# Windowed attention feeding a mixture of experts on one core: transposes two steps ahead, one mask, routing in small pieces, two experts' weights picked from the biases

## The chip, the core and the metric

The kernel runs on one core of a Trainium2 chip. A core has a matrix engine (TensorE, PE in the profile; its weight loads are PEld), a vector engine (VectorE, DVE), an activation engine (ScalarE, ACT), a general engine (GpSimd, POOL) and a queue engine that only starts transfers (SyncE, SP). Each engine runs its own instructions strictly in program order, and semaphores make one wait for another. SP, ACT and POOL can each start DMA transfers. The metric is the device time of one launch in microseconds (us); lower is better. Three timed runs give the median, and one further execution was profiled.

## The reference

Attention with a window of 32 positions to either side, over 8 batches, 8 heads, 576 positions and 64 values per head, then a mixture of 8 experts in which each of the 4608 tokens goes to one expert only:

```python
scores = scale * q @ k.T            # per batch and head, [576, 576]
scores = where(abs(i - j) <= 32, scores, -1e9)
x = softmax(scores) @ v             # then [4608, 512], heads side by side
logits = x @ w_gate + modality_bias[modality_id]
e = argmax(logits); gate = softmax(logits)[e]
out[token] = gate * (relu(x @ w1[e]) @ w2[e])
```

`w1` is 8 x 512 x 1024 and `w2` is 8 x 1024 x 512, all in fp32; `modality_bias` is 2 x 8 and spread widely, so that in these inputs the modality of a token mostly decides its expert.

## The kernel before, in words

The whole program is written out by hand in one order (`tc.manual_schedule()`), and each engine follows that order. The attention is worked in 32 steps, `it = 4*b + hp`: one batch `b` and one pair of heads `hp` in each. Eight more steps (`it` 32 to 39) have no attention. A step of the loop at L725 emits, in this order:

- at its head, the loads of batch b+2 (`load_main`, `load_rest` on the SP queue at hp 0; `load_v`, L129, on the ACT queue, at hp 1 and hp 3) and the casts to bf16 of batch b+1, nearly all on POOL (`pool_cast`, L111);
- at hp 1, `logits` of batch b-1 (L361) and `best` (L374, seven short DVE operations and an exponential);
- `scores(it+1, 0)` (L226): four matmuls of key slots 0 and 1 for the two heads, whose keys lie on partitions 0 to 63 and 64 to 127. Each slot of 128 keys meets 192 queries. The moving operand is read out of `q_t`, which holds the positions in four interleaved rows (`[P, NH, R, WP]`), so that neighbouring columns of the matmul lie 304 bytes apart. An exponential on ACT (L242) and a product with the mask on DVE (L244) follow;
- one `work(1)`, then `scores(it+1, 2)` for slots 2 and 3 and a last slot of 96 queries with a mask of its own (L250);
- at hp 0, pieces of `x_tr` (transposes of the finished batch); at hp 2, `tr_rest` (L206), the transposes of the last 64 positions;
- one `work(1)`, then `values(it)` (L253): 18 short matmuls, a reciprocal and a product on DVE that writes `xt` (L272);
- at hp 1, `place` (L397), for the first batch also `choose` (L527), and `dispatch` (L555): some twenty short DVE operations in a row, that say where each token goes; POOL then scatters the tokens to a scratch in HBM (L423);
- two more `work(1)`, and between them `tr_main(it+2)` (L215): eight transposes into one PSUM tile, a copy to `k_t` on ACT (L222) and one to `q_t` on DVE (L224). `scores` of the next step reads both and is the next thing on PE.

`work(n)` takes n units off a list. A unit is a quarter of an expert's first product (`up`, L472: eight matmuls of 256 columns and a relu on ACT) or of its second (`down`, L482: four of 512; every second one ends with DVE's `ys`, L491, and a scatter by POOL to the output, L494). A tile of 256 tokens begins with `turn` (L458): transposes, a copy on ACT (L466), the output rows on DVE. Two tiles are put on the list after each batch, of the two experts that `choose` found among the tokens of batch 0. `choose` also starts the loads of these two experts' weights on POOL's queue (L434; four transfers, read as 2 MB of fp32 each, written as 1 MB of bf16).

Before the loop, PE's first instruction is the transpose of the modality numbers (L331), which come by five DMAs on the SP queue (L325) behind the loads of batch 1. After the loop, `table` (L601, 33 short DVE operations) lays out the remaining tokens of all experts in tiles, `zero` is written behind each expert's rows, and three such tiles are worked in `tail` (L798).

PSUM is full: one score tile of two banks, one output tile of two, two transpose buffers (`ps_t`, shared by `tp`, `tpr`, `tpx`, `tpf`, `rk`), one each for `up` and `down`.

Of the kernel before, what the change touches and what calls it, by code (L numbers as in the profile page):

```python
# [31 lines left out]
def kernel(  # L32
# [27 lines left out]
    PD = 8  # L60
    WP = PD + S // R
# [16 lines left out]
    ldv = ctx.enter_context(tc.tile_pool(name="ldv", bufs=8))  # L78
# [44 lines left out]
    def load_rest(b):  # L123
        rf = ldr.tile([SR, 2, H, D], FP32, tag="rf", name="rf")
        nc.sync.dma_start(rf[:, 0], q[b, :, SM:S, :].rearrange("h s d -> s h d"))
        nc.sync.dma_start(rf[:, 1], k[b, :, SM:S, :].rearrange("h s d -> s h d"))
        Ld[b, "r"] = rf

    def load_v(b, js):  # L129
        for j in js:  # L130
            s0 = P * j if j < NM - 1 else S - P
            p0 = 0 if j < NM - 1 else P - SR
            f_ = ldv.tile([P, H, D], FP32, tag="vf", name="vf")
            nc.scalar.dma_start(f_[p0:P], v[b, :, s0 + p0:s0 + P, :].rearrange("h s d -> s h d"))
            Ld[b, "v", j] = f_
# [11 lines left out]
    def cast_rest(b):  # L147
        rb = ldr.tile([SR, 2, HD], BF16, tag="rb", name="rb")
        pool_cast(rb[:], Ld[b, "r"][:].rearrange("p u h d -> p u (h d)"))
        Ct[b, "r"] = rb  # L150

    def cast_v(b, js):
        for j in js:
            p0 = 0 if j < NM - 1 else P - SR
            pool_cast(v_t[b % 2][p0:P, j, :, 0:D], Ld[b, "v", j][p0:P])
# [3 lines left out]
    load_v(0, range(NM))  # L159
# [6 lines left out]
    WIN, WL = 192, 96  # L166
    SW = 256
    PW = 4 * SW + P

    q_t = [const.tile([P, NH, R, WP], BF16, name=f"qT{i}") for i in range(2)]  # L170
    k_t = [const.tile([P, NH, S], BF16, name=f"kT{i}") for i in range(2)]
    p_t = [const.tile([P, 2, PW], BF16, name=f"pt{i}") for i in range(2)]
    v_t = [const.tile([P, NM, H, D + 1], BF16, name=f"vt{i}") for i in range(2)]
    x_t = [const.tile([P, NM, ROW // 2], I32, name=f"xt{i}") for i in range(2)]

    def prep(i):
        nc.vector.memset(q_t[i][:, :, :, 0:PD], 0.0)
        nc.vector.memset(v_t[i][:, :, :, D:D + 1], 1.0)
        nc.vector.memset(v_t[i][0:P - SR, NM - 1, :, 0:D], 0.0)
        pv = p_t[i][:, :, 0:4 * SW].rearrange("p h (j c) -> p h j c", c=SW)  # L180
# [34 lines left out]
    def tr_main(it):  # L215
# [629 lines left out]
```

## Time and profile before

| | us |
|---|---|
| median of 3 runs (lowest, highest) | 446.59 (444.91, 449.06) |
| the profiled execution, its own time | 444.8 |
| its span, from the first to the last instruction | 443.2 |
| PE busy in it | 293.3 (66%) |
| DVE, ACT, POOL busy | 167.4, 163.4, 157.4 |
| mean granted TensorE clock | 0.85 of full |

The span is what the trace shows, and 1.6 us of the execution lie around it. [...]

### The profile page before, as it was taken

What the parts mean: (1) busy time and instruction counts of PE and PEld (TensorE: products, weight loads), DVE (VectorE), ACT (ScalarE), POOL (GpSimd) and SP (SyncE); (2) the same over time, 40 slices, a digit from 0 to 9 for tenths busy, and PEclk for the clock granted to TensorE, in tenths of its full rate; (3) what the DMA queues carried; (4) which work ended last, traced back from release to release, by engine and by line L of the source; (5) the groups of instructions that cost most, each with busy time, mean ns of one, the idle gap of its engine ahead of it and who ended that gap; (6) DMA issues with size and microseconds to landing.
All of it is one profiled execution on the core that took longest, in us unless ns stands there. A gap on an engine that the chain in (4) does not pass through costs nothing. (4 is left out here: it accounts for less than half of the span.)

```text
span 443.2 us, 7071 instructions
## 1 busy us (share of the span) xinstructions
PE 293.3 (66%) x2649; PEld 182.6 (41%) x2649; DVE 167.4 (38%) x523; ACT 163.4 (37%) x274; POOL 157.4 (36%) x216
## 2 busy tenths in 40 slices
PE   0015765406877898787888788898888877068730
PEld 0013444204644554454455445455556544045410
DVE  2015445603354455336335533644543312601110
ACT  0204354204643444454355435455535323023300
POOL 1824340823035327353642633381161611002120
PEclk9999997555988588898889888889989989569985
DMA  9999431399917823940692260240032221621020
GB/s 194 271 211 289 131 74 36 85 224 237 253 44 202 204 60 92 292 140 25 179 262 61 77 152 26 68 147 24 26 108 98 84 95 71 226 76 49 24 75 1
DMA packets 79353, 55.34 MB, mean 125 GB/s; under 512 B 49192, under 2 KB 74832, under 8 KB 79312
## 3 DMA queue, kind: packets, MB, share of 16 engines
q1 hardware_dynamic: 33184, 26.72, 22.5%
q0 software_dynamic: 8624, 18.66, 14.6%
q10 hardware_dynamic: 37504, 9.44, 10.6%
q8 instruction: 22, 0.36, 0.4%
q14 instruction: 19, 0.16, 0.1%
HBM read 54.64 MB, written 18.04 MB: 164 GB/s over the span
## 5 line engine op out<-in xcount | busy, mean ns | idle before, releaser
L478 PE MATMUL ph<-xTf,w 128*128 128x256 bf16 x608 | 87.0, 291 | 20.1 <-ACT xTf L466 14.1
L237 PE MATMUL st<-qT,kT 64*128 64x192 bf16 (+1 forms) x320 | 57.2, 459 | 57.6 <-DVE qT L224 29.6
L487 PE MATMUL py<-w,hT 128*128 128x512 bf16 x304 | 89.8, 425 | 2.2 <-DMA w<-in_moe_w_dram 1.3
L244 DVE TENSOR_TENSOR pt<-pt,mask 128x768 bf16<-128x768 bf16 x64 | 40.2, 627 | 117.6 <-ACT pt L242 117.6
L242 ACT ACTIVATE pt<-st 128x768 bf16<-128x768 f32 x64 | 51.8, 810 | 82.8 <-PE st L237 58.8
L478 PEld LDWEIGHTS <-w 128*128 128x128 bf16 x608 | 60.1, 104 | 45.9 <-issue 29.2
L494 POOL DMA_INDIRECT out_dram<-ys,ix x38 | 37.3, 983 | 111.8 <-DVE ys L491 59.5
L480 ACT ACTIVATE hT<-ph 128x512 bf16<-128x512 f32 x76 | 45.2, 595 | 85.7 <-PE ph L478 85.7
L423 POOL DMA_INDIRECT scr<-xt,di x40 | 40.9, 1023 | 72.2 <-DVE ro L566 47.2
L491 DVE TENSOR_SCALAR ys<-py,xg 128x512 f32<-128x512 f32 x38 | 28.3, 745 | 62.5 <-PE py L487 61.9
L237 PEld LDWEIGHTS <-kT 64*128 64x128 bf16 x320 | 16.0, 102 | 81.2 <-issue 68.0
L111 POOL TENSOR_SCALAR cb<-qkf 128x1024 bf16<-128x1024 f32 x30 | 31.3, 1065 | 44.5 <-PE tp L221 31.5
L487 PEld LDWEIGHTS <-hT 128*128 128x128 bf16 x304 | 29.5, 105 | 33.7 <-issue 14.6
L111 POOL TENSOR_SCALAR vt<-vf 128x512 bf16<-128x512 f32 (+1 forms) x40 | 25.7, 664 | 27.8 <-issue 15.6
L261 PEld LDWEIGHTS <-pt 128*128 128x128 bf16 x320 | 27.4, 117 | 10.0 <-issue 7.5
L466 ACT COPY xTf<-tpf 128x1024 bf16<-128x1024 bf16 x19 | 19.3, 1016 | 28.0 <-PE tpf L463 27.9
L261 PE MATMUL ot<-vt,pt 128*128 128x65 bf16 x320 | 29.3, 221 | 0.0
L266 PE MATMUL ot<-vt,pt 128*128 128x65 bf16 x256 | 27.6, 220 | 0.0
L222 ACT COPY kT<-tp 128x512 bf16<-128x512 bf16 x32 | 18.8, 586 | 22.7 <-PE tp L221 22.7
L272 DVE TENSOR_TENSOR xt<-ot,rec 128x640 bf16<-128x640 f32 x32 | 26.4, 824 | 1.2
L358 ACT COPY xTr<-tpx 128x512 bf16<-128x512 bf16 x40 | 23.1, 586 | 5.0 <-PE tpx L356 5.0
L463 PE MATMUL tpf<-ident,xg 128*128 128x128 bf16 x152 | 12.9, 233 | 18.1 <-DVE ix L468 14.6
(145 smaller groups left out, 266.0 us busy)
## 6 DMA issues: line engine op xcount, KB each, us to landing
w<-in_moe_w_dram POOLq DMA_DIRECT2D x10, 1024.0 KB, 29.9
qkf<-in_q_dram SPq DMA_DIRECT2D x16, 512.0 KB, 6.9
vf<-in_v_dram ACTq DMA_DIRECT2D x32, 256.0 KB, 4.5
qkf<-in_k_dram SPq DMA_DIRECT2D x16, 512.0 KB, 8.4
xg<-scr SPq DMA_DIRECT2D x19, 272.0 KB, 3.3
scr<-zero SPq DMA_DIRECT2D x9, 272.0 KB, 2.8
rf<-in_q_dram SPq DMA_DIRECT2D x8, 128.0 KB, 16.7
rf<-in_k_dram SPq DMA_DIRECT2D x8, 128.0 KB, 10.1
```

Of the source, the lines that this page charges most:

```text
L111: nc.gpsimd.tensor_scalar(out=o_ap, in0=i_ap, scalar1=1.0, scalar2=0.0, op0=ALU.mult, op1=ALU.add)
L237: nc.tensor.matmul(st[:, h, c0:c0 + w_], k_t[b % 2][D * h:D * h + D, hp, k0:k0 + P], q_t[b % 2][D * h:D * h + D, hp, :, q0:q0 + w_ // R].r ...
L242: nc.scalar.activation(p_ap, st[:, :, 0:2 * WIN].rearrange("p h (j c) -> p h j c", c=WIN), ACT.Exp, scale=scale)
L244: nc.vector.tensor_tensor(out=p_ap, in0=p_ap, in1=mask[:].unsqueeze(1).to_broadcast([P, 2, 2, WIN]), op=ALU.mult)
L261: nc.tensor.matmul(o_ap, pt[:, h, SW * m:SW * m + P], vt[:, m, 2 * hp + h, :], start=(m == 0), stop=(m == 0), skip_group_check=True)
L266: nc.tensor.matmul(o_ap, pt[:, h, c1:c1 + P], vt[:, m - 1, 2 * hp + h, :], start=False, stop=True, skip_group_check=True)
L423: ins = nc.gpsimd.indirect_dma_start(out=scr[:], out_offset=bass.IndirectOffsetOnAxis(ap=di[:, m:m + 1], axis=0), in_=xi[:, m, :], in_offs ...
L478: nc.tensor.matmul(ph[:, u, :], w1[:, kd, P * mi:P * mi + P], self.xT[:, kd, :], start=(kd == 0), stop=(kd == n_kd - 1))
L480: nc.scalar.activation(self.hT[:, 2 * mp:2 * mp + 2, :], ph[:], ACT.Relu)
L487: nc.tensor.matmul(self.py[:], self.hT[:, kf, P * s:P * s + P], w2[:, kf, :], start=(kf == 0), stop=(kf == n_kf - 1))
L491: nc.vector.tensor_scalar(out=ys[:], in0=self.py[:], scalar1=self.xg[:, s, HD // 2:HD // 2 + 1].bitcast(FP32), scalar2=None, op0=ALU.mult)
L494: ins = nc.gpsimd.indirect_dma_start(out=out, out_offset=bass.IndirectOffsetOnAxis(ap=self.ix[:, s:s + 1], axis=0), in_=ys[:], in_offset=N ...
```

## The change

Seven things are done together.

1. `q_t` holds the positions in their natural order, with 32 columns of zeros ahead and behind; the copy out of PSUM undoes the interleaving. All five key slots are aligned alike, and the last one is computed with 128 queries and keys padded by zeros.
2. The mask is one `[P, 192]` pattern, multiplied once in a step over all ten slots of the two heads (`masking`), after `values` of the step before.
3. `tr_main(it+2)` stands right behind `scores(it+1, 0)` instead of near the end of the step, and uses one PSUM buffer for keys and one for queries. `tr_rest` transposes queries and keys together (four transposes of 128 rows instead of eight of 64).
4. `best`, `place` and `dispatch` yield after each DVE operation, and `trickle` emits 3, 3, 2 and 3 of them at four places of a step, over some two and a quarter steps; `table` is emitted in the same way in steps 36 to 38.
5. The two experts of the in-loop tiles are the argmax of each modality's bias, known at the start: `load_ab(0)` starts two of the weight loads ahead of the loop, `load_ab(1)` the other two at step 1. `choose` is gone.
6. The modality numbers and biases are loaded first thing on the ACT queue; their transpose stands behind the first scores (`make_bias`). The values `v` of batches 1 to 7 are loaded on the SP queue. The write of the zero rows (`zp_ins`) goes from the SP queue to the ACT queue.
7. Units are not worked before step 10 (`W0`); tiles are fetched and put on the list at hp 3; the tail fetches a tile ahead of the units that remain.

The diff, cut to what the prediction speaks of:

```diff
     def load_rest(b):
+        rf = ldr.tile([P, H, D], FP32, tag="rf", name="rf")
+        nc.sync.dma_start(rf[0:SR], q[b, :, SM:S, :].rearrange("h s d -> s h d"))
+        nc.sync.dma_start(rf[SR:P], k[b, :, SM:S, :].rearrange("h s d -> s h d"))
...
+    def load_v(b, eng):
+        for j in range(NM - 1):
+            eng.dma_start(f_[:, j], v[b, :, P * j:P * j + P, :].rearrange("h s d -> s h d"))
+        eng.dma_start(l_[:], v[b, :, SM:S, :].rearrange("h s d -> s h d"))
...
     load_main(0, 0)
     load_rest(0)
-    load_v(0, range(NM))
+    mb_bc = const.tile([P, n_mod, E], FP32)
+    nc.scalar.dma_start(mb_bc[:], moe_modality_bias.partition_broadcast(P))
...
+        nc.scalar.dma_start(mid64[B * m:B * m + B, p0:p1], idv[:, s0 + p0:s0 + p1])
+    load_v(0, nc.scalar)
     load_main(0, 1)
...
-    q_t = [const.tile([P, NH, R, WP], BF16, name=f"qT{i}") for i in range(2)]
+    q_t = [const.tile([P, NH, QP + S + QP], BF16, name=f"qT{i}") for i in range(2)]
...
     def tr_main(it):
         b, hp = divmod(it, NH)
         g, l = hp // 2, 2 * (hp % 2)
-        tp = ps_t.tile([P, 2, R, P], BF16, tag="tp", name="tp")
         for u in (1, 0):
+            tp = ps_t.tile([P, R, P], BF16, tag="tp", name=f"tp{u}")
             for i in range(R):
-                nc.tensor.transpose(tp[:, u, i, :], Ct[b, g, u][:, i, D * l:D * l + P], ident[:])
-        nc.scalar.copy(k_t[b % 2][:, hp, 0:SM].rearrange("d (c r) -> d c r", r=R),
-                       tp[:, 1].rearrange("d r c -> d c r"))
-        nc.vector.tensor_copy(q_t[b % 2][:, hp, :, PD:PD + P], tp[:, 0])
+                nc.tensor.transpose(tp[:, i, :], Ct[b, g, u][:, i, D * l:D * l + P], ident[:])
+            i_ap = tp[:].rearrange("d r c -> d c r")
+            if u:
+                nc.scalar.copy(k_t[b % 2][:, hp, 0:SM].rearrange("d (c r) -> d c r", r=R), i_ap)
+            else:
+                nc.vector.tensor_copy(q_t[b % 2][:, hp, QP:QP + SM].rearrange("d (c r) -> d c r", r=R), i_ap)
...
-                    q_t[b % 2][D * h:D * h + D, hp, :, q0:q0 + w_ // R].rearrange("d r c -> d c r"),
-                    start=True, stop=True)
+                    q_t[b % 2][D * h:D * h + D, hp, P * j:P * j + w_], start=True, stop=True)
...
+    def masking(it):
+        p_ap = p_t[it % 2][:].rearrange("p h (j c) -> p (h j) c", c=SW)[:, :, 0:WIN]
         nc.vector.tensor_tensor(
+            out=p_ap, in0=p_ap, in1=mask[:].unsqueeze(1).to_broadcast([P, 2 * NM, WIN]), op=ALU.mult)
...
-    zp_ins = nc.sync.dma_start(scr[ZP:ZP + TT, :].rearrange("(s p) c -> p s c", p=P), zero[:])
+    zp_ins = nc.scalar.dma_start(scr[ZP:ZP + TT, :].rearrange("(s p) c -> p s c", p=P), zero[:])
...
+    step = [0]
+    W0 = 2 * NH + 2
     def work(n):
-        while units and (n > 0 or units[0][0].__name__ == "turn"):
+        while units and step[0] >= W0 and (n > 0 or units[0][0].__name__ == "turn"):
...
+    for i, m_ in ((0, 0), (1, n_mod - 1)):
+        nc.vector.tensor_reduce(out=pm[:, i:i + 1], in_=mb_bc[:, m_, :], axis=AX.X, op=ALU.max)
+        nc.vector.tensor_scalar(out=pe[:, i, :], in0=mb_bc[:, m_, :], scalar1=pm[:, i:i + 1], scalar2=None,
+                                op0=ALU.is_equal)
+    nc.vector.tensor_tensor(out=pe[:], in0=pe[:], in1=io_e8[:].unsqueeze(1).to_broadcast([P, 2, E]), op=ALU.mult)
+    nc.vector.tensor_reduce(out=pm[:], in_=pe[:], axis=AX.X, op=ALU.min)
...
+    def load_ab(i):
+        e_r = reg(sp_i[0:1, i:i + 1], [ET.Pool], 0, E - 1)
+        load_w(1, i, e_r)
+        load_w(2, i, e_r)
...
+    def route(b):
+        yield from best(b)
+        ranks(b)
+        yield from place(b)
+        yield from dispatch(b)
...
     scores(0, 0)
     scores(0, 2)
+    masking(0)
+    cast_main(0, 1, split=True)
+    load_ab(0)
+    make_bias()
     for it in range(n_it + 2 * NH):
...
+        if it == 1:
+            load_ab(1)
         st = None
         if hp == 1 and rb is not None:
             st = logits(rb)
+            chain[0] = route(rb)
         if it + 1 < n_it:
             scores(it + 1, 0, st)
+        if hp == 2 and it + 2 < n_it:
+            tr_rest(b + 1)
+        if it + 2 < n_it:
+            tr_main(it + 2)
+        trickle(3)
         work(1)
         if it + 1 < n_it:
             scores(it + 1, 2)
         if hp == 0 and rb is not None:
+            x_tr(rb, 0)
             x_tr(rb, 1)
+        trickle(3)
         work(1)
+        if live:
+            values(it)
         if hp == 0 and rb is not None:
             x_tr(rb, 2)
+        if it + 1 < n_it:
+            masking(it + 1)
+        trickle(2)
         work(1)
         if hp == 0 and rb is not None:
             x_tr(rb, 3)
+            x_tr(rb, 4)
+        trickle(3)
         work(1)
+        if hp == 3 and rb is not None:
+            trickle(99)
             for t in got[rb]:
                 t.fetch()
             for t in got[rb]:
                 enqueue(t)
+            if rb == B - 1:
+                chain[0] = table()
+    trickle(99)
...
     def tail(idx, first):
+            t.fetch()
+            work(len(units))
             load_w(1, i % 2, e_r, cond=(c_r == 1))
+            load_w(2, i % 2, e_r, cond=(c_r == 1))
             enqueue(t)
```

## Rows read from the trace of the kernel before

**Rows 1.** The page's span in 40 equal slices: PE's busy tenths

```profile
PE   0015765406877898787888788898888877068730
```

**Rows 2.** Timeline of the start: start us, us, engine, line, operation, [idle before <-releaser]

```profile
20.18 0.19 POOL L302 CAST iof<-ioi 128x8 f32<-128x8 int32 x1
...
22.32 0.56 POOL L345 MEMSET zero<- 128x544 int32 x1
...
31.03 0.21 PE L331 MATMUL midp<-ident,midr 40*128 40x40 bf16 x1 [31.03 <-DVE midr L327]
...
34.84 0.81 PE L237 MATMUL st<-qT,kT 64*128 64x192 bf16 x4
```

**Rows 3.** Timeline of `xt`, written once a step: steps 0, 3, 9 and 31

```profile
43.13 0.82 DVE L272 TENSOR_TENSOR xt<-ot,rec 128x640 bf16<-128x640 f32 x1
...
61.09 0.82 DVE L272 TENSOR_TENSOR xt<-ot,rec 128x640 bf16<-128x640 f32 x1
...
124.99 0.82 DVE L272 TENSOR_TENSOR xt<-ot,rec 128x640 bf16<-128x640 f32 x1
...
332.47 0.82 DVE L272 TENSOR_TENSOR xt<-ot,rec 128x640 bf16<-128x640 f32 x1
```

**Rows 4.** Timeline, steps 5 to 7: the stall at the weight loads

```profile
80.98 0.82 PE L237 MATMUL st<-qT,kT 64*128 64x192 bf16 x4 [6.38 <-DVE qT L224]
...
84.61 0.86 POOL L438 DMA_DIRECT2D w<-in_moe_w_dram  x1
...
86.22 14.05 ACTq L134 DMA_DIRECT2D vf<-in_v_dram  x3
...
101.17 0.98 PE L237 MATMUL st<-qT,kT 64*128 64x192 bf16 x6 [12.34 <-ACT pt L242]
```

**Rows 5.** The view of tile `w` to 130 us: issue to landing of four loads

```profile
DMA to landing us min/median/max: 26.3/29.9/33.5
```

**Rows 6.** Windows: length, busy (count) of PE PEld DVE ACT POOL, PEclk, DMA, GB/s

```profile
0.00:31.00 31.00, 0.00 (x0) 0.00 (x0) 2.90 (x15) 3.37 (x3) 14.11 (x50) 1.00 1.03 222
31.00:72.00 41.00, 27.48 (x271) 17.92 (x273) 21.41 (x47) 18.49 (x31) 13.52 (x16) 0.99 0.62 158
...
135.00:345.00 210.00, 176.39 (x1680) 107.85 (x1678) 97.64 (x305) 99.03 (x172) 87.68 (x99) 0.88 0.42 118
```

**Rows 7.** Windows again, one of 2 us that holds a score group

```profile
80.00:82.00 2.00, 0.82 (x4) 0.25 (x4) 0.86 (x6) 0.17 (x1) 1.70 (x2) 0.50 0.33 122
```

**Rows 8.** Waits of PE alone from 135 to 345 us: total, times, longest

```profile
PE st L237 <- DVE qT L224: 12.6, 15, 1.7
PE ph L478 <- ACT xTf L466: 8.4, 6, 1.5
PE st L237 <- ACT pt L242: 5.7, 4, 2.0
```

**Rows 9.** Timeline of PE in step 27, at full clock

```profile
298.85 0.22 PE L261 MATMUL ot<-vt,pt 128*128 128x65 bf16 x2
...
299.40 1.03 PE L478 MATMUL ph<-xTf,w 128*128 128x256 bf16 x8
...
300.27 0.61 PE L221 MATMUL tp<-ident,cb 128*128 128x128 bf16 x8
...
302.05 0.81 PE L237 MATMUL st<-qT,kT 64*128 64x192 bf16 x4 [0.31 <-DVE qT L224]
```

**Rows 10.** Groups of instructions, shapes apart: busy us, mean ns, idle before

```profile
L244 DVE TENSOR_TENSOR pt<-pt,mask 128x768 bf16<-128x768 bf16 x64 | 40.2, 627 | 117.6 <-ACT pt L242 117.6
...
L224 DVE COPY qT<-tp 128x512 bf16<-128x512 bf16 x32 | 13.5, 421 | 20.0 <-ACT kT L222 19.7
...
L381 DVE TENSOR_TENSOR oh<-lo,mx 128x40 f32<-128x40 f32 x8 | 1.6, 200 | 0.3
```

**Rows 11.** Timeline of the end: after the table, and the last scatter

```profile
390.20 1.01 PE L463 MATMUL tpf<-ident,xg 128*128 128x128 bf16 x8 [14.58 <-DVE ix L468]
...
427.71 0.97 POOL L494 DMA_INDIRECT out_dram<-ys,ix  x1 [1.75 <-POOLq L814]
```

More of the change, by code (lines that the diff above doesn't have):

```diff
@@ L405, in place @@
                 start=False, stop=(m == NM - 1), skip_group_check=True)
+    def place(b):
+        xi, ohb, rk = x_t[b % 2], Ct[b, "oh"], Ct[b, "rk"]
         pos = rt.tile([P, E], FP32, tag="pos", name="pos")
@@ L556, in dispatch @@
+    got = {}
+    def dispatch(b):
         cm = small.tile([P, 2, E], FP32, tag="cm", name="cm")
@@ L718, with trickle, run_all @@
     n_it = NH * B
-    got = {}
+    chain = [None]
+    def trickle(n):
+        while chain[0] is not None and n > 0:
+            if next(chain[0], chain) is chain:
+                chain[0] = None
+            n -= 1
+    def run_all(g):
+        for _ in g:
+            pass
+    def route(b):
[3 more added lines that the diff above has]
+        yield from dispatch(b)
     tr_rest(0)
@@ L759 @@
         if hp == 0 and rb is not None:
+            x_tr(rb, 0)
             x_tr(rb, 1)
-        if hp == 2 and it + 2 < n_it:
-            tr_rest(b + 1)
+        trickle(3)
         work(1)
+        if live:
+            values(it)
         if hp == 0 and rb is not None:
             x_tr(rb, 2)
-        if live:
-            values(it)
-        if hp == 1 and rb is not None:
-            place(rb)
-            if rb == 0:
-                choose()
-            got[rb] = dispatch()
+        if it + 1 < n_it:
+            masking(it + 1)
+        trickle(2)
         work(1)
@@ L775 @@
             x_tr(rb, 3)
-        if it + 2 < n_it:
-            tr_main(it + 2)
+            x_tr(rb, 4)
+        trickle(3)
         work(1)
-        if hp == 0 and rb is not None:
-            x_tr(rb, 4)
-        if hp == 2 and rb is not None:
+        if hp == 3 and rb is not None:
+            trickle(99)
             for t in got[rb]:
                 t.fetch()
-        if hp == 3 and rb is not None:
             for t in got[rb]:
                 enqueue(t)
-    tab_steps = table()
-    while units:
-        work(1)
-        for _ in range(4):
-            next(tab_steps, None)
-    for _ in tab_steps:
-        pass
+            if rb == B - 1:
+                chain[0] = table()
+    trickle(99)
     tab, pen_i = T["tab"], T["pen"]
@@ L804, in tail @@
             load_w(1, i % 2, e_r, cond=(c_r == 1))
-            t.fetch()
+            load_w(2, i % 2, e_r, cond=(c_r == 1))
             enqueue(t)
-            work(len(units))
-            load_w(2, i % 2, e_r, cond=(c_r == 1))
+        work(len(units))
         for n in range(4):
```

244 lines of the change are left out of this document (115 added, 129 removed).

## The prediction

> **What bounds the kernel now.** I read the page's 40 slices first. PE is idle for nearly three of them at the start, has a hole in slices 7 to 9 and one near the end; between them it is busy eight to nine tenths [rows 1]. So there are four terms: start, early hole, main loop, end.
>
> At the start PE's first instruction waits 31 us for the modality numbers, and all other PE work is queued behind it; the first scores begin at 34.84 [rows 2]. In the hole, ACT needs 14.05 us to issue three loads of `v` while the weight loads fill the DMA engines; its exponential is behind them, and PE waits 12.34 us for that [rows 4]. In step 6 PE also waited 6.38 us for the copy of q, which stood behind `place`, `choose` and `dispatch` on DVE [rows 4]. In the loop a step takes (332.47 - 124.99)/22 = 9.43 us [rows 3]. From 135 to 345 us PE is idle for 210 - 176.39 = 33.6 us, 1.55 in a step of 9.69 (210/9.69 = 21.7 steps); ACT is busy for 99.03/21.7 = 4.6 us of a step, DVE 4.5, POOL 4.0 [rows 6]. [...] At the end PE is idle 14.58 us while DVE works the table [rows 11].
>
> **The change, part by part**, against the profiled span of 443.2 us.
>
> *Start.* The transpose of the modality numbers leaves PE's head. What is late next: ACT now has to issue `zp_ins` ahead of its first copy of k, and that waits for `zero`, which POOL has done at 22.32 + 0.56 = 22.9 [rows 2]; behind ACT's wait stand all copies of k and exponentials. DVE has the choice of experts ahead of its first copy: some 12 small operations at 0.20 [rows 10] behind an index table that POOL makes at 20.18 + 0.19 [rows 2], so 22.8. Both say 22.9 (20 if POOL's queue gets shorter by the two masks and the cast that leave it, 28 if `v` lands later). From there two rounds of transposes and copies through two PSUM buffers take some 2.4 us: first scores at 25.3, not 34.84. From first scores to `xt` of step 0 it was 43.13 - 34.84 = 8.3; less 2 for faster scores and one wait for q, plus some 0.5 as ACT's cast of the second half of k now stands there: 6.7. `xt` of step 0 comes at 32 (29 to 37).
>
> *Steps 1 to 9.* They took (61.09 - 43.13)/3 = 5.99 each before any routing [rows 3]. Less 0.9 for scores and 0.6 for the wait for q (both below): 4.5, bounds 4.0 and 5.5. `xt` of step 9 is at 32 + 9 x 4.5 = 72.5. Do the transfers allow it? In the first 31 us come 31 x 222 GB/s = 6.9 MB, about two batches (3.54 MB each), so 15 us a batch [rows 6]. The weights take at most 33.5 us from 84.61 [rows 4, 5], in which one whole batch comes too: 33.5 - 15 = 19. Three batches and the weights are 64 us, and the first third of batch 3 makes 69: it just fits. I add 2 us for order, since SP's fetch of the first tiles is queued behind batch 3's `v`: 74.5 (0 to +12). Before it was 124.99, with 8 units done by then that are now still to do. `work` is gated to step 10, so the weights have until then. The issue of `v` goes from ACT, where it cost 14.05, to SP, where only loads and fetches stand behind it.
>
> *Main loop, steps 10 to 31.*
> (a) Scores. Four matmuls of 192 columns take 0.81 at full clock [rows 9] and 0.82 at a granted clock of 0.50 [rows 4, 7], six 0.98 [rows 4]. What doesn't change with PE's clock isn't the array; I take it to be the strided read of q. `up` streams 8 x 256 columns in 300.27 - 299.40 = 0.87, or 0.42 ns a column, plus a tail of 1.03 - 0.87 = 0.16 [rows 9]. At that rate, with both heads at once, the groups take 0.32 and 0.38; one head after the other, 0.48 and 0.60; if it isn't the stride, nothing is gained. The saving is 1.09, 0.71 or 0; I take 0.9 a step.
> [...] No run here shows a contiguous score matmul.
> (b) Waits. Of PE's listed waits, 12.6 us for q, 8.4 for `xTf`, 5.7 for the exponential [rows 8], the first goes (12.6/21.7 = 0.58 a step): the copy now has a whole step's time, and routing is no longer ahead of it in one piece. The exponential gets the eight transposes as cover beside one unit; half of its 0.26 and half of the 0.39 for `xTf` go. Together -0.9, bounds 0 and -1.55 (all idle time).
> (c) Clock. [...] As far as lows come from the waits that go: -0.4 (0 to -1.1).
> (d) Added. DVE's copy of q now reads PSUM with a stride: from 0.42 as before to, at most, the 0.63 of the larger mask product [rows 10]. One mask of 1920 elements against two of 768 and a short one: at most 0.627 x 2.5 = 1.57 against 1.25 and more, so nothing to speak of. DVE stays under 5 us, POOL loses little, ACT is unchanged in sum, but at hp 0 five copies of `xTr` and one of `xTf` meet, and the two PSUM buffers change hands 17 times in a batch instead of 13. I add 0.3 (0 to 1).
> 9.43 - 0.9 - 0.9 - 0.4 + 0.3 = 7.5 (bounds 5.8 and 10.4; I hold 6.5 to 8.8 for likely, as PE's work alone is near 6). 22 x 7.5 = 165: `xt` of step 31 at 239.5.
>
> *Steps 32 to 39.* They took 390.20 - 14.58 - 332.47 = 43.1 [rows 3, 11] with 28 units (16 tiles make 124, 96 were done before). Now 32: + 4 x 0.87, and about 5 less for waits on tiles and low clock: 41.6 (38 to 46). The table's operations lie beside units.
>
> *End.* The 14.58 go (at least 9 of them); some 1 us of register loads on PE stays, and 4 units are left, 3.5. From the first tail tile to the last scatter 427.71 - 390.20 = 37.5, and 443.2 - 427.71 = 15.5 after it [rows 11], both as before.
>
> Sum: 74.5 + 165 + 41.6 + 1 + 3.5 + 37.5 + 15.5 = 338.6; with 1.6 around the span 340.2, where the profiled execution had 444.8. The median of the runs is 0.4% above that one: 341.
>
> **Rivals.**
> *A, the loop stays coupled:* q's wait goes but PSUM hand-over and ACT's crowd at hp 0 take its place, a step of 8.6. 22 x 1.1 more: 365. For: buffers change hands more often; against: ACT is busy 4.6 of 9.7 [rows 6].
> *B, the early transfers are late:* the weights crowd out batches 1 and 2, as they held up `v` in [rows 4]; steps 4 to 9 wait, some 12 us: 353. Against: the 69 us above.
> [...]
> *D, nothing comes of it:* gains at start and end are eaten by a step slower than before (at some 12.3 us, should routing in pieces hold up masks and values at each place): within 1%.
>
> **How the numbers follow.** Forecast 0.70, A 0.15, B 0.10, C 0.03, D 0.02. The likeliest is 341; its parts (start and early steps -10 to +15, loop -22 to +28, rest -7 to +7) added in squares make 316 to 372, which takes in B and most of A. About 1% is what a measurement here can tell from no change: faster 0.95, within 1% 0.02, slower 0.03.
>
> **What would show it.** First scores near 25, behind ACT's wait for `zero`; `xt` of step 9 near 74 and no wait of ACT on its own DMA issues; score groups near 0.35 and 0.4; no wait of PE for `qT`; `xt` 7.5 apart; PE's idle before the tail under 4 us. The forecast is wrong if score groups stay at 0.8, if the granted clock falls below 0.8 in the loop, or if steps 4 to 9 wait for loads.

## The result, and the profile of the changed kernel

The changed kernel took 348.74 us (median of 4 runs, 346.44 to 350.13) where the kernel before, beside it, took 446.66: a ratio of 0.780, with a 95% interval of 0.774 to 0.786. The forecast was 341, with a range of 316 to 372. The profiled execution has a span of 348.4 us against 443.2, that is 94.8 less.

The page's 40 slices first, PE's busy tenths and the granted clock:

```profile
PE   0114776535779897988889798798398688888810
...
PEclk9999998655599999999999999999699999999975
```

A slice is now 8.7 us. PE is idle for most of the first three, 24 us of 26, where before it was 32 of 33 [rows 1]; the hole before the tail is gone; the early hole is still there, in slices 7 to 10, and the granted clock is at its lower level, 0.50, in slices 9 to 11 (of the 480 half-microsecond windows from 60 to 300 us 397 show 1.00, 78 show 0.50 and 5 a value between). There is a new hole, in slice 29 (244 to 253 us, step 31): ACT's copy, and PE's wait for it.

```profile
248.14 1.01 ACT L478 COPY xTf<-tpf 128x1024 bf16<-128x1024 bf16 x1 [3.07 <-remote]
...
249.21 1.87 PE L490 MATMUL ph<-xTf,w 128*128 128x256 bf16 x8 [5.43 <-ACT xTf L478]
```

The transposes that this copy reads had ended at 243.77. The experiments come back to this ("The changed kernel again").

`xt`, the last DVE operation of a step's values, divides the span as in [rows 3]. Its timeline: steps 0, 7, 8, 9, 23 and 31.

```profile
36.33 0.82 DVE L272 TENSOR_TENSOR xt<-ot,rec 128x640 bf16<-128x640 f32 x1
...
64.66 0.82 DVE L272 TENSOR_TENSOR xt<-ot,rec 128x640 bf16<-128x640 f32 x1
...
79.08 0.82 DVE L272 TENSOR_TENSOR xt<-ot,rec 128x640 bf16<-128x640 f32 x1 [2.19 <-DMA scr<-xt,di]
...
85.65 0.83 DVE L272 TENSOR_TENSOR xt<-ot,rec 128x640 bf16<-128x640 f32 x1
...
194.04 0.82 DVE L272 TENSOR_TENSOR xt<-ot,rec 128x640 bf16<-128x640 f32 x1
...
253.88 0.82 DVE L272 TENSOR_TENSOR xt<-ot,rec 128x640 bf16<-128x640 f32 x1
```

Steps 0 to 7 are (64.66 - 36.33)/7 = 4.05 us apart, but step 8 comes 14.4 after step 7, and step 10, in which the first units are worked, 13.2 after step 9. Against [rows 3], 39.3 of the 94.8 us are won up to step 9, 39.3 in the 22 steps from 9 to 31 (a mean of 7.65 a step, not 9.43, step 10 among them), and 16.2 behind it.

Windows of the loop, columns as in [rows 6], and PE's longest waits in the same stretch (total, times, longest):

```profile
105.00:243.00 138.00, 121.21 (x1465) 82.91 (x1462) 91.17 (x225) 86.72 (x152) 70.76 (x78) 1.00 0.53 151
```
```profile
PE tpx L349 <- DVE qT L227: 3.9, 4, 1.0
PE tp L222 <- DVE kT L214: 3.3, 4, 0.8
```

The wait of the scores for `qT`, 12.6 us in [rows 8], has left the list. The two waits that lead it now are of transposes for a PSUM buffer that a copy on DVE has to set free; together they are 7.2 us, 0.38 a step. The granted clock is 1.00 where it was 0.88; PE is idle 0.88 us of a 7.26 us step (16.8 us in 138/7.26 = 19 steps), not 1.55. A score group in this stretch, four and then six matmuls, where [rows 9] had 0.81 for the four:

```profile
156.57 0.34 PE L238 MATMUL st<-qT,kT 64*128 64x192 bf16 x4
...
158.93 0.40 PE L238 MATMUL st<-qT,kT 64*128 64x192 bf16 x6
```

The end: the first tail tile's transposes, without a wait where [rows 11] had 14.58, and the last scatter.

```profile
298.33 0.61 PE L475 MATMUL tpf<-ident,xg 128*128 128x128 bf16 x8
```
```profile
333.02 0.97 POOL L506 DMA_INDIRECT out_dram<-ys,ix  x1 [1.76 <-POOLq L860]
```

### The profile page after: what moved, and what is told of

It reads as the page before. It is cut to its first block, busy times and chain, and to the rows that moved or that the text cites. A ratio compares the mean times of both kernels' runs of the same rounds, so it can differ in the third digit from the quotient of the medians.

```text
span 348.4 us, 6915 instructions
## 1 busy us (share of the span) xinstructions
PE 242.0 (69%) x2617; PEld 165.7 (48%) x2617; DVE 173.8 (50%) x464; ACT 162.4 (47%) x274; POOL 149.9 (43%) x195
## 5 line engine op out<-in xcount | busy, mean ns | idle before, releaser
L490 PE MATMUL ph<-xTf,w 128*128 128x256 bf16 x608 | 81.8, 278 | 22.4 <-ACT xTf L478 9.8
L499 PE MATMUL py<-w,hT 128*128 128x512 bf16 x304 | 79.4, 383 | 3.5 <-DVE ys L503 2.2
L222 PE MATMUL tp<-ident,cb 128*128 128x128 bf16 x256 | 25.5, 243 | 26.0 <-DVE kT L214 12.9
L250 DVE TENSOR_TENSOR pt<-pt,mask 128x1920 bf16<-128x1920 bf16 x32 | 37.8, 1182 | 2.4 <-ACT pt L245 2.4
L271 DVE RECIPROCAL rec<-ot 128x10 f32<-128x10 f32 x32 | 7.0, 219 | 58.9 <-PE ot L266 29.6
L222 PEld LDWEIGHTS <-cb 128*128 128x128 bf16 x256 | 17.2, 108 | 33.8 <-DVE kT L214 14.3
L238 PE MATMUL st<-qT,kT 64*128 64x192 bf16 (+1 forms) x320 | 26.2, 261 | 9.9 <-DVE lo L363 3.6
L227 DVE COPY qT<-tp 128x512 bf16<-128x512 bf16 x32 | 22.0, 689 | 17.4 <-PE tp L222 16.4
L261 PE MATMUL ot<-vt,pt 128*128 128x65 bf16 x320 | 24.3, 202 | 5.7 <-POOL vt L110 5.3
L261 PEld LDWEIGHTS <-pt 128*128 128x128 bf16 x320 | 22.4, 103 | 7.6 <-issue 1.3
L225 ACT COPY kT<-tp 128x512 bf16<-128x512 bf16 x32 | 18.8, 586 | 15.4 <-POOL le L606 11.6
L478 ACT COPY xTf<-tpf 128x1024 bf16<-128x1024 bf16 x19 | 19.2, 1012 | 13.2 <-PE tpf L475 10.1
```

What stands on the lines that cost most here:

```text
L222: nc.tensor.transpose(tp[:, i, :], Ct[b, g, u][:, i, D * l:D * l + P], ident[:])
L250: nc.vector.tensor_tensor(out=p_ap, in0=p_ap, in1=mask[:].unsqueeze(1).to_broadcast([P, 2 * NM, WIN]), op=ALU.mult)
L261: nc.tensor.matmul(o_ap, pt[:, h, SW * m:SW * m + P], vt[:, m, 2 * hp + h, :], start=(m == 0), stop=(m == 0), skip_group_check=True)
L490: nc.tensor.matmul(ph[:, u, :], w1[:, kd, P * mi:P * mi + P], self.xT[:, kd, :], start=(kd == 0), stop=(kd == n_kd - 1))
L499: nc.tensor.matmul(self.py[:], self.hT[:, kf, P * s:P * s + P], w2[:, kf, :], start=(kf == 0), stop=(kf == n_kf - 1))
```

## The experiments

They ran in three groups, each beside the kernel before on its own chip, which took 450.28, 441.92 and 441.08 us there. So ratios are compared, and the third group has the changed kernel itself once more.

**The changed kernel again.** No edit. It ran in the last group, but belongs first, since the others are read by it.

> The changed kernel as it is, run beside the three that follow. In its first profile a batch of the loop took 29.3 us, with 9.3 to 9.7 us for the last step of each batch; in the four kernels of the last comparison (table, weights, casts of v, biases) a batch took 26.4 us or 27.3, with 6.1 us for that step, whatever had been edited, and they ran on another chip. Theory (that difference is the chip's and no edit's): the changed kernel itself shows either 29.3 us and a ratio near 0.78, or 26.4 us a batch and 330 to 334 us, a ratio of 0.75 to 0.757, and the three kernels beside it show the same batch. Rival (each of those edits freed the loop in its own way): 29.3 us here and less in the others.

331.62 us (329.98 to 335.09), ratio 0.758 (0.752 to 0.764): the second form of the theory, with a ratio just above the 0.757 put down. The same program is 17 us faster on this chip, where the kernel before gained 5.6. A batch takes 26.5 us and not 29.3, as in three of the four kernels of the second group. `xt` of steps 9 and 31 in this trace:

```profile
85.68 0.83 DVE L272 TENSOR_TENSOR xt<-ot,rec 128x640 bf16<-128x640 f32 x1
...
235.44 0.82 DVE L272 TENSOR_TENSOR xt<-ot,rec 128x640 bf16<-128x640 f32 x1
```

Step 23, the last of its batch, in the first trace and in this one: GpSimd's last scatter of five, the last of the values' 18 matmuls, then DVE's reciprocal that waits for it.

```profile
190.27 0.97 POOL L435 DMA_INDIRECT scr<-xt,di  x1 [0.30 <-issue]
```
```profile
190.31 0.20 PE L266 MATMUL ot<-vt,pt 128*128 128x65 bf16 x1
```
```profile
193.78 0.22 DVE L271 RECIPROCAL rec<-ot 128x10 f32<-128x10 f32 x1 [4.47 <-PE py L499]
```
```profile
183.73 0.97 POOL L435 DMA_INDIRECT scr<-xt,di  x1 [0.30 <-issue]
```
```profile
183.77 0.20 PE L266 MATMUL ot<-vt,pt 128*128 128x65 bf16 x1
```
```profile
184.00 0.22 DVE L271 RECIPROCAL rec<-ot 128x10 f32<-128x10 f32 x1 [1.96 <-PE ot L266]
```

In the second trace DVE starts at once when the values end, at about 183.97. In the first it starts 3.3 us after them, and 3.2 to 3.6 us late in the last step of each of the four batches from step 12 to 27, while GpSimd issues the scatters. ACT is held up alike: its copy in step 31 begins 4.4 us after the transposes that it reads [the row at 248.14]. There the profile names the releaser "remote": it finds no instruction of this core that released it. This name stands on ACT or DVE in the first trace and in all four of the first group, and in none of the eight traces of the other two groups. The scatters themselves run alike (0.97 us each, 1.27 apart). What holds up the signal the traces don't show. From step 9 to 31 the two traces differ by 168.23 - 149.76 = 18.5 us, 2.9 in each of those four batches and 5.8 in the last one; up to step 9 (85.7 in both) and behind step 31 (94.5 and 94.9) they agree. The kernels of the first group have the long last step of a batch too (9.1 us with q strided, for 9.3 in the first trace and 6.1 in this one), so they are compared with 0.780; the second and third group have the short one and are compared with 0.758.

**q strided again.**

```diff
-q_t = [const.tile([P, NH, QP + S + QP], BF16, ...
+q_t = [const.tile([P, NH, R, (QP + S + QP) // R], BF16, ...
...
-    q_t[b % 2][D * h:D * h + D, hp, P * j:P * j + w_], ...
+    q_t[b % 2][D * h:D * h + D, hp, :, P // R * j:(P * j + w_) // R].rearrange("d r c -> d c r"),
```

> The changed kernel with q stored again in four interleaved rows, so that the right-hand side of every score matmul is strided and the copy of q out of PSUM is contiguous. All else as in the changed kernel: both heads in one group of four and one of six matmuls. Theory (the stride is what made the old score groups long, and they stand on TensorE's path): the groups of four and of six go from 0.34 and 0.39 us to about 0.80 and 0.97, so some 1.0 us per step, in the 22 steps from 10 to 31 alone 23 us (the first ten steps wait for transfers and hide it): 372 us, from 366 to 378. Rival 1 (it was the one-head-after-another order that was slow, not the stride): groups stay under 0.5 and the time within 4 us of 348.7. Rival 2 (the stride costs TensorE time, but the loop is bound elsewhere): groups long and the time under 358.

360.32, ratio 0.801 (0.797 to 0.804): 0.021 x 446.7 = 9 us lost. Added to 348.7 that is 358, the second rival's bound and not the theory's 366 to 378. The groups are just as the theory has them:

```profile
162.36 0.81 PE L239 MATMUL st<-qT,kT 64*128 64x192 bf16 x4
...
164.72 1.02 PE L239 MATMUL st<-qT,kT 64*128 64x192 bf16 x6
```

So the stride alone made them long, by 0.81 + 1.02 - 0.34 - 0.40 = 1.09 us a step: the order of the heads has no part in it. But from step 9 to 31 it costs 177.5 - 168.2 = 9.3 us, 0.42 a step. The steps at hp 1 and hp 2 grow by 1.1 and 0.6 us; the one that holds the late signal and the one behind it don't grow at all (9.1 for 9.3, and 5.3). On a chip without that lateness this wasn't tried.

**Contiguous q alone, in the kernel before.**

```diff
-q_t = [const.tile([P, NH, R, WP], BF16, ...
+q_t = [const.tile([P, NH, R * WP], BF16, ...
...
-    q_t[b % 2][D * h:D * h + D, hp, :, q0:q0 + w_ // R].rearrange("d r c -> d c r"),
+    q_t[b % 2][D * h:D * h + D, hp, R * q0:R * q0 + w_],
```

> The kernel before with one part of the change alone: q stored in natural order, so that the right-hand sides of the score matmuls are contiguous, and the copy of q out of PSUM strided. Transposes, routing, masks, weights and table as before. Theory (parts add up): about 1.0 us per step off TensorE in the 22 steps from 10 to 31, and little in the steps that wait for transfers: 446.6 - 23 = 424, from 418 to 432; the wait for qT grows by the 0.27 us by which the strided copy is longer. Rival (before, the loop had slack from its waits, so that a shorter group only lengthens a wait): 440 to 447.

437.27, ratio 0.971 (0.967 to 0.975): 13 us won, a little over half of what was expected, between theory and rival. Windows and PE's wait, from 135 to 345 us as in [rows 6, 8]:

```profile
135.00:345.00 210.00, 154.22 (x1662) 108.01 (x1681) 103.81 (x308) 98.68 (x172) 89.95 (x99) 0.89 0.40 114
```
```profile
PE st L238 <- DVE qT L224: 24.6, 14, 3.8
```

PE is busy 154.22 us, 22 less than before, but waits 24.6 for `qT`, 12 more. The work that left PE had been cover for the copy of q, and the copy itself is longer (0.69 us for 0.42, some 4 of the 12 us over 14 waits). In this trace the 22 steps from 9 to 31 take 207.5 us, as many as before [rows 3]: on PE the loop's work shrank and its waits grew by as much. What the traces show as won is 6.3 us up to step 9 (118.67 for 124.99) and 1.6 behind the loop. The kernel before has no trace on this chip, where it took 3.6 us longer, so how much of the 13 is the loop's stays open. That this part counts in full with the transposes out of the way isn't shown either.

**Transposes at their old place.**

```diff
-        if it + 2 < n_it:
-            tr_main(it + 2)
         trickle(3)
...
             x_tr(rb, 3)
+        if it + 2 < n_it:
+            tr_main(it + 2)
```

> The changed kernel with the transposes of q and k, and those of the rest rows, at their old places: tr_main(it + 2) behind the fourth x_tr near the end of the step, tr_rest behind the second half of the scores. Theory (the wait for qT stands between TensorE and the next scores): the wait of the scores for qT comes back with about 0.6 us per step, and with it some of the idle time between units: 22 steps by 0.6 to 0.9 = 13 to 20 us, so 365 (360 to 372). Rival (with the routing spread, VectorE is free when the copy comes, and the copy is done in time wherever it stands): within 4 us of 348.7.

393.23, ratio 0.866 (0.862 to 0.871): 0.086 x 446.7 = 39 us lost, more than twice what was expected, and the largest of the parts that were undone. (The profiled execution took 397.81, at a mean clock of 0.868 where three others had 0.89 to 0.90, so its terms are somewhat too large.) Windows of the start and the loop of this kernel, and of the start of the changed one, then a wait in step 1 of this kernel:

```profile
0.00:100.00 100.00, 39.81 (x467) 31.48 (x468) 47.34 (x113) 34.97 (x57) 42.79 (x73) 0.83 1.03 229
110.00:290.00 180.00, 142.18 (x1541) 97.80 (x1563) 97.07 (x242) 96.46 (x165) 79.28 (x85) 0.89 0.43 121
```
```profile
0.00:100.00 100.00, 46.01 (x569) 33.77 (x570) 51.23 (x135) 40.98 (x68) 52.03 (x83) 0.83 1.07 241
```
```profile
45.04 0.50 PE L238 MATMUL st<-qT,kT 64*128 64x192 bf16 x4 [2.86 <-DVE qT L227]
```

(`tr_rest` went back behind the second half of the scores as well.) A step from 0 to 7 takes (85.2 - 35.7)/7 = 7.1 us and not 4.05; from 36 to 86 us PE waits for `qT` six times, 14.2 us in all, where the changed kernel waits 0.6. From step 9 to 31 it is (301.9 - 101.1)/22 = 9.1. PE's longest waits from 110 to 290 us:

```profile
PE tp L222 <- ACT kT L225: 10.6, 5, 2.3
PE st L238 <- DVE qT L227: 9.5, 7, 3.1
```

So the wait for `qT` comes back with 0.48 us a step (180/9.1 = 19.7 steps), near the theory's 0.6, but more is lost where the transposes wait for ACT's copy of k to set a buffer free. The granted clock of the loop is 0.89, as in the kernel before, where the changed kernel has 1.00. From 115 to 240 us PE has six waits of 1.9 to 4.4 us, and the clock's six stretches at 0.50 each begin in one of them or shortly behind it, so waits and low clock come together. In the first trace the clock's falls near 65.5 and 246.5 us lie in waits of PE too, of 3.13 and 5.43 us.

**Routing in two pieces.**

```diff
-            chain[0] = route(rb)
         if it + 1 < n_it:
             scores(it + 1, 0, st)
+        if st is not None:
+            run_all(best(rb))
...
             masking(it + 1)
+        if st is not None:
+            ranks(rb)
+            run_all(place(rb))
+            run_all(dispatch(rb))
```

> The changed kernel with the routing of a batch in two pieces again: the choice of the expert right behind the first half of the scores, ranks, places and dispatch behind the values of the same step. Theory (a block of some 20 small VectorE operations in the hp = 1 step holds up the copies of q and the masks): about 5 us of VectorE work in one piece, of which 2 to 4 us per batch come onto the path, 6 batches inside the loop: 361 (356 to 370). Rival (the block is covered by the units): within 4 us of 348.7. A second rival: the scatters leave a step earlier and the casts of v behind them on GpSimd with them, so that it is faster, 340 to 345.

365.26, ratio 0.809 (0.805 to 0.813): 0.029 x 446.7 = 13 us lost, the theory's size. A batch takes 34.2 us and not 29.3, and the step that grows is the one after the block, hp 2: 10.9 for 7.4. There, GpSimd's first scatter, ACT's and PE's wait:

```profile
191.95 1.00 POOL L435 DMA_INDIRECT scr<-xt,di  x1 [6.30 <-issue]
```
```profile
200.67 0.60 ACT L492 ACTIVATE hT<-ph 128x512 bf16<-128x512 f32 x1 [6.44 <-remote]
```
```profile
202.22 0.58 PE L222 MATMUL tp<-ident,cb 128*128 128x128 bf16 x4 [4.88 <-ACT xTf L478]
```

The relu waits for a releaser that the profile names "remote", 4.95 to 6.44 us, four times in the loop; in the row shown, the matmuls that it reads had ended at 195.44. GpSimd issues the scatters meanwhile, and PE waits 4.88 behind it. So the size was right, but the wait is not the theory's: DVE's block is done at 192.3 (`thr`, its last short operation), and the stall is a late signal during the scatters, as in the first trace. Whether the 13 us are there on a chip without that lateness wasn't tried, and so the cause stays open.

**The table behind the loop.**

```diff
             if rb == B - 1:
-                chain[0] = table()
+    chain[0] = table()
     trickle(99)
```

> The changed kernel with the table of the tail worked out in one piece behind the loop's last units, where the kernel before had most of it, and not spread between them from step 35 on. Theory (the table's small VectorE operations, some 40, and the register loads behind them stand between the last units and the tail when nothing covers them): the 14.58 us of idle time of the kernel before come back in large part, +9 to +14, a ratio to the kernel before of 0.805 (0.798 to 0.814) where the changed kernel has 0.781. Rival (the tail waits for its weights anyway, so the table is hidden behind a transfer): ratio under 0.787.

343.05, ratio 0.777 (0.769 to 0.785). Against 0.780 it would look like nothing; a batch takes 26.5 us here, so it stands against 0.758 and is a loss, 0.0187 x 441 = 8 us. Step 31 ends at 235.4 in this trace and in that of the changed kernel's second run, and the last scatter begins at 326.15 and 315.08: 11 us, the theory's. PE's wait in front of the last four units, ahead of the first tail tile:

```profile
285.26 1.86 PE L490 MATMUL ph<-xTf,w 128*128 128x256 bf16 x8 [8.14 <-DVE g L725]
```

Behind it the four units run at a granted clock of 0.51 (285 to 291 us) and take 1.3 to 1.9 us each and not 1.03, which makes most of the rest of the 11.

**Weights at steps 4 and 5.**

```diff
-    load_ab(0)
...
-        if it == 1:
-            load_ab(1)
+        if it in (4, 5):
+            load_ab(it - 4)
```

> The changed kernel with the weights of the two experts asked for at steps 4 and 5 and not at the start and at step 1. In the changed kernel the 16 DMA engines are full from 26 to 100 us (busy share above 1 in both stretches), and the ninth and the eleventh step came 14.4 and 13.2 us after the one before. Theory (the weights, 8 MB read by the second step, push back the loads of batch 2, and these end the waits of steps 8 to 10): step 9 ends at about 76 and not 85.7, and as the weights then land at about 85 to 90, close to the first unit, the gain is kept in part: ratio 0.765 (0.755 to 0.775). Rival 1 (every byte is wanted by step 10 in either order): the wait moves from the steps to the first units, ratio 0.776 to 0.787. Rival 2 (the weights come too late and the units stall as in the kernel before): ratio above 0.79.

333.66, ratio 0.760 (0.754 to 0.766), the changed kernel's 0.758: no gain. First the changed kernel, in its first trace DVE's index for the scatters of batch 0 and the first of these, in its second the cast of v ahead of them; then this kernel, the first scatter, the values of step 8, and `xt` of steps 8 and 9.

```profile
59.72 0.17 DVE L426 TENSOR_SCALAR di<-dr 128x5 int32<-128x5 f32 x1
...
67.89 1.10 POOL L435 DMA_INDIRECT scr<-xt,di  x1 [0.29 <-POOL xt L433]
```
```profile
63.99 1.05 POOL L110 TENSOR_SCALAR vt<-vf 128x1024 bf16<-128x1024 f32 x1 [8.94 <-DMA vf<-in_v_dram]
```
```profile
60.33 1.10 POOL L435 DMA_INDIRECT scr<-xt,di  x1 [6.80 <-DVE rec L271]
...
68.47 0.19 PE L261 MATMUL ot<-vt,pt 128*128 128x65 bf16 x1 [2.14 <-POOL vt L110]
...
80.30 0.82 DVE L272 TENSOR_TENSOR xt<-ot,rec 128x640 bf16<-128x640 f32 x1 [10.22 <-DMA scr<-xt,di]
...
86.87 0.82 DVE L272 TENSOR_TENSOR xt<-ot,rec 128x640 bf16<-128x640 f32 x1
```

86.9 and not 76: the gain that the theory wanted doesn't come. But the weights matter all the same. In the changed kernel the index is ready at 59.9, but GpSimd waits with the cast of batch 2's v, whose load lands late beside the weights, until 63.4, has casts of q and k behind it, and starts the scatters at 67.9. Here that cast comes at 47.4, the scatters start at 60.3 and the values of step 8 at 68.5, for 75.3. Then `xt` waits 10.22 us for these scatters, which now run beside the weights: the three whose landing the trace has took 13.8 to 18.6 us, for 4.6 to 6.7 in the changed kernel's second trace. So one wait takes the place of the other. Weights out of the way of both the loads and the scatters weren't tried. Read against 0.780 the ratio alone would have confirmed the theory.

**Casts of v ahead of the scatters.**

```diff
         if hp == 1 and nb is not None:
             cast_rest(nb)
-            cast_v(nb, 0)
+            cast_main(nb, 1)
         if hp == 2 and nb is not None:
-            cast_main(nb, 1)
-        if hp == 3 and nb is not None:
+            cast_v(nb, 0)
             cast_v(nb, 1)
             cast_v(nb, 2)
```

> The changed kernel with the casts on GpSimd in another order: those of q and k a step earlier at most, those of v all at the third step of a batch, ahead of the five scatters of the batch before, where two of the three stood behind them. Theory (the values of step 8 waited 5.1 us for a cast of v that stood behind five scatters of 1.28 us, though its load had landed, and steps 10 and the last of every batch look alike): 4 to 8 us, nearly all of it ahead of step 11: ratio 0.767 (0.76 to 0.773). Rival 1 (the loads land late anyway and the wait takes their name): ratio 0.777 to 0.785. Rival 2 (a cast of v waits for its load ahead of casts of q and k, and holds up the transposes): slower, ratio above 0.787.

338.33, ratio 0.767 (0.762 to 0.773), against 0.758 a loss of 4 us: a batch takes 27.3 us and not 26.5, the step at hp 1 8.0 and not 7.2. First the changed kernel's step 8: the fifth scatter of batch 0, the cast of v behind it, the values, and `xt`; then `xt` of step 8 in this kernel.

```profile
73.17 0.97 POOL L435 DMA_INDIRECT scr<-xt,di  x1 [0.31 <-issue]
74.17 1.07 POOL L110 TENSOR_SCALAR vt<-vf 128x1024 bf16<-128x1024 f32 x1
```
```profile
75.29 0.21 PE L261 MATMUL ot<-vt,pt 128*128 128x65 bf16 x1 [5.07 <-POOL vt L110]
```
```profile
80.09 0.82 DVE L272 TENSOR_TENSOR xt<-ot,rec 128x640 bf16<-128x640 f32 x1 [10.24 <-DMA scr<-xt,di]
```

The wait for the cast (5.07) is gone, and another takes its name: `xt` of step 8 writes the buffer that the scatters of batch 0 read, and waits 10.24 us until they have landed, at 80 us, among full transfers. In the changed kernel that wait was 2.19 [the row at 79.08].

**Biases at step 2.**

```diff
-    make_bias()
 for it in range(n_it + 2 * NH):
...
+        if it == 2:
+            make_bias()
```

> The changed kernel with the modality biases worked out at step 2 and not in the start, where their five VectorE operations (31.6 to 35.3 us) stood between the first mask and the first copies of q of the loop, and held a PSUM buffer of the transposes for 2.4 us. Theory (the start is a chain, and what leaves it comes off the end): xt(0) at 33 and not 36.3, ratio 0.773 (0.77 to 0.776). Rival (the steps from 4 on wait for transfers, so that an earlier start ends in a longer wait): xt(0) earlier all the same, step 9 where it was, ratio 0.778 to 0.785.

332.51, ratio 0.755 (0.750 to 0.760): no difference from 0.758. `xt` of steps 0 and 9:

```profile
33.67 0.82 DVE L272 TENSOR_TENSOR xt<-ot,rec 128x640 bf16<-128x640 f32 x1
...
86.20 0.82 DVE L272 TENSOR_TENSOR xt<-ot,rec 128x640 bf16<-128x640 f32 x1
```

The start is 2.6 us shorter than the 36.33 of the changed kernel, and step 9 stands where it was: the rival's outcome, but not by its wait alone. The biases now lengthen step 2 to 8.3 us (3.4 in the changed kernel), so that step 3 is already late, at 48.1 for 45.7.

**Three buffers for the attention output.**

```diff
-x_t = [const.tile([P, NM, ROW // 2], I32, name=f"xt{i}") for i in range(2)]
+x_t = [const.tile([P, NM, ROW // 2], I32, name=f"xt{i}") for i in range(3)]
...
-        xi, ohb, rk = x_t[b % 2], Ct[b, "oh"], Ct[b, "rk"]
+        xi, ohb, rk = x_t[b % 3], Ct[b, "oh"], Ct[b, "rk"]
```

> The changed kernel with three buffers for the attention output x_t where it has two. With the casts of v ahead of the scatters, the normalisation of step 8 waited 10.24 us for the scatters of batch 0, which read the buffer that it writes and landed near 80 us among the full transfers; in the changed kernel that wait is 2.2 us, since the values of step 8 came late themselves behind the casts of v. Theory (two waits end at nearly the same time, so that taking away one gives what lies between them): xt(8) 1.5 to 2.5 us earlier, and the time by 0 to 2.5 less than the changed kernel beside it. Rival (the buffer is the only bound): xt(8) near 70 and 8 us less.

330.73, ratio 0.757 (0.752 to 0.762), 0.9 us under the changed kernel beside it: within the theory and within the measurement's spread. `xt` of step 8 comes at 77.0; the values still wait for the cast.

**Three buffers and the casts of v first.** Beside the three buffers:

```diff
         if hp == 2 and nb is not None:
             cast_main(nb, 1)
-        if hp == 3 and nb is not None:
             cast_v(nb, 1)
             cast_v(nb, 2)
```

> Three buffers for x_t, and the second and third cast of v one step earlier, ahead of the five scatters on GpSimd. Theory (both waits of step 8 are gone, and what is late next are the loads of batch 3 and the first fetch, near 80): xt(8) at 70 to 73 and not 79, xt(9) at 77 to 80 and not 86, and as TensorE isn't idle for 10 us there its clock stays at the higher level; 5 to 9 us less than the changed kernel beside it. Rival 1 (all bytes wanted by step 10 end at the same time whatever waits for them): xt(8) earlier, xt(11) where it was, within 2 us of the changed kernel. Rival 2 (the casts delay the scatters by 1.7 us in every batch, and these the fetches): slower by 1 to 4 us.

331.79, ratio 0.762 (0.755 to 0.769): nothing won, as the first rival has it, though `xt` of step 8 comes at 70.2. Step 9 comes 12.5 us later. Its DVE, GpSimd and PE:

```profile
75.43 6.11 DVE L384 TENSOR_TENSOR oh<-iof,mi 128x40 f32<-128x40 f32 x1
```
```profile
75.83 2.08 POOL L110 TENSOR_SCALAR cb<-qkf 128x1024 bf16<-128x1024 f32 x2
...
79.44 2.04 POOL L110 TENSOR_SCALAR cb<-qkf 128x1024 bf16<-128x1024 f32 x2
```
```profile
82.60 0.21 PE L403 MATMUL rk<-ohb,tri 128*128 128x40 bf16 x1 [7.01 <-DVE ohb L388]
```

A DVE operation that takes 0.20 us elsewhere lasts 6.11, beside six casts in a row on GpSimd (four of them in the rows), from 75.83 to 81.48; PE waits 7.01 behind it. So a third wait was ready to end at nearly the same time. `xt` of step 9 is 3 us earlier, at 82.7, and the loop afterwards gives nothing more.

**And the biases at step 2 with them.**

> As the kernel with three buffers and the casts of v a step earlier, and the modality biases at step 2 and not in the start. Theory (what the start gives is lost again in the steps that wait for transfers): xt(0) 2 to 3 us earlier, the time within 1.5 us of the kernel without this part. Rival (with the waits of step 8 gone the early chain counts): 2 to 4 us less than it.

329.48, ratio 0.757 (0.751 to 0.762): 2.1 us under the changed kernel beside it and 2.3 under the one without this part, the rival's size in the medians; but the intervals overlap with both, so it can't be called faster. `xt` of step 9 is at 84.7, 2 us later than without it, so no early chain shows in the trace.

## Why the prediction was right, and which step failed

The forecast was 2% under the time, and the time lies well inside the range. In part that is luck, as told under the loop. Its terms for the first chip against the trace of the changed kernel:

| term | forecast | measured |
|---|---|---|
| `xt` of step 9 | 74.5 | 85.65 |
| 22 steps to step 31 | 165 | 168.2 |
| from there to the first tail tile | 41.6 + 1 + 3.5 = 46.1 | 298.33 - 253.88 = 44.45 |
| tail, to the last scatter | 37.5 | 333.02 - 298.33 = 34.7 |
| after it | 15.5 | 348.4 - 333.02 = 15.4 |

*Start: right in place, short in size.* First scores came at 26.64 for 25.3, behind ACT's first copy of k:

```profile
25.06 0.58 ACT L225 COPY kT<-tp 128x512 bf16<-128x512 bf16 x1 [11.60 <-POOL le L606]
```

The profile names POOL's `le` for this wait, but ACT issues the write of `zero` at 24.62, right ahead of the copy and right after POOL has made `zero` (24.04 + 0.55), so it is the wait that was forecast, 1.7 us later. `xt` of step 0 came at 36.33 for 32: the biases' DVE operations were moved into this chain, which the step didn't count, and moving them out gives 2.6 of the 4.3 us back (biases at step 2).

*Steps 1 to 9: the step that failed.* "It just fits. I add 2 us for order" was mis-sized: 11 us more at step 9, near the +12 of its upper bound. Up to step 7 the steps ran at 4.05, under the forecast 4.5. The bytes came about as counted: the forecast has three batches and the weights in by 64 us, and GpSimd casts batch 2's first v at 63.45 (63.99 in the second trace). What the step put at nothing is the work between that landing and the values of step 8, all in GpSimd's order: casts of q and k, the five scatters of batch 0, which had waited for GpSimd since 59.9, and the other casts of v. That makes 75.29 - 63.45 = 11.8 us. Then `xt` waits 2.19 more until the scatters have landed. So rival B had the size and a part of the cause: weights asked for 15 us later bring the values of step 8 forward by 6.8 us, but step 9 stays at 86.9, since the scatters then land late. Taken away one by one the waits replace each other (weights later, casts first, three buffers), and with the last two both gone DVE's wait at GpSimd comes third.

*Loop: right in the sum, by luck in part.* The 168.2 us hold the late signals, for which the forecast has no term. On the chip without them the same 22 steps took 149.8, 15 us less than the forecast's 165 and 6.8 a step (the kernel before was 5.6 us faster there too). So the parts (a) to (d) together were put too low, and a loss that nobody foresaw filled the gap.

*(a) Scores: 0.9 a step, measured 1.06 to 1.09 on PE* (0.34 and 0.39 or 0.40 us, the "both heads at once" end of the bound), settled by the strided q. Six matmuls took 0.39 or 0.40 us, where the forecast's estimate was 0.38 with both heads at once and 0.60 one after the other. Four took 0.34 us, and 0.81 with the stride. The strided four took as long at either clock (0.81 and 0.82 in the kernel before); the contiguous four take 0.34 at a granted clock of 1.00 and 0.51 at 0.50 (first trace, at 60.64 us). On the end of the kernel it is worth 0.42 a step on the first group's chip.

*(b) and (c), waits and clock: -1.3 a step, measured about -1.5* by the transposes at their old place (9.1 against 7.65, of which some 0.2 to 0.3 is the longer execution that was profiled). The forecast had them as two terms; in that trace they come together. No run shows the clock's -0.4 by itself; the granted clock of the loop went from 0.88 to 1.00, and is 0.89 with the transposes at their old place. Of the waits only 0.48 a step is for `qT`, and the largest is for a PSUM buffer, which the forecast had as rival A. The 9.69 us step by which the forecast divides stands in no row; with the 9.43 of [rows 3] the wait for q is 0.57 a step and not 0.58. The same waits cost 3 us a step in steps 0 to 7, where only 0.6 was put down.

*(d) Added: +0.3.* The copy of q takes 0.69 us, just over the bound of 0.63, the mask at most what was bounded. That the routing in pieces saves 13 us had no term of its own. Two sums of the forecast are a little off, without effect: the lower bound of a step is 5.7 and not 5.8, and the range's upper end 373.5 and not 372.

The parts don't add: undone singly, stride, transposes, routing and table cost 9 + 39 + 13 + 8 to 11, some 70 us (the table on another chip than the rest), where all together won 98, and contiguous q alone gave 13 where its undoing costs 9. What one part takes away is cover for the wait of another.

*End: right.* The 14.58 are gone, and the table behind the loop brings 8.14 of them back.

Rival A (a step of 8.6) did not come: the step is 7.65; its hand-over of PSUM buffers is there, but at 0.38 us a step. Nor did D, whose step of 12.3 is the one at which the 446.6 - 341 = 105.6 us of the forecast are used up in 22 steps (7.5 + 4.8), nor C of the chances, a slower loop: the granted clock is 1.00 in it, for 0.88 before.

## What to carry to other kernels

Work taken off the bounding engine pays in full only if nothing was waiting under its cover: contiguous q alone doubled the wait for the copy of q (24.6 us for 12.6) and, in its trace, left the loop as long as it was. In a stretch bound by transfers count what has to happen after a load has landed, and the scatters too: where they stand in the issuing engine's order and which buffer their landing sets free. And expect two or three waits to end within a few microseconds of each other. Run the unedited kernel in the same group: without it, the table would have passed for hidden here, and weights, casts and biases for gains.

## What the hardware showed that was not expected

**The same program on another chip.** The loop took 168.2 and 149.8 us. In the last step of each batch DVE starts 3.2 to 3.6 us after the values that PE's records show finished, while GpSimd issues five scatters, and in step 31 ACT is late by 4.4 us. Why is open. Such waits are in the first trace and in all of the first group, and in none of the eight traces of the other two chips.

**DVE behind GpSimd.** Operations of 0.17 to 0.20 us lasted 1.68 us beside two casts in a row (four batches of the changed kernel), 2.68 beside three and 6.11 beside six (three buffers and the casts of v first).

```profile
182.27 1.68 DVE L426 TENSOR_SCALAR di<-dr 128x5 int32<-128x5 f32 x1
```

One of each kind ended at 183.95, 175.41 and 81.54 us, and the casts beside it at 183.92, 175.38 and 81.48. So the operation lasted until the whole row of casts was through, up to six of them. What held it the traces don't show.
